# Top-32 attention with a transformer channel block: a deeper score lead, spread loads, one value transfer per job and an earlier vector transpose

## The chip, the core and the metric

The kernel runs on one core of one Trainium2 chip. A core has five engines that run their own instruction streams in order and meet only at semaphores: PE (TensorE, matrix products), DVE (VectorE), ACT (ScalarE), POOL (GpSimd) and SP (SyncE, which here only issues transfers). Transfers run on 16 DMA engines. The metric is the device time of one execution in microseconds, lower is better. The kernel before was run three times: 1655.44, 1657.19 and 1660.09 us, median 1657.19.

## The reference

The inputs are q, k, v of shape (8 batches, 8 heads, 576 rows, 64 columns) in float32, a layer-norm gain in float32 and two weights in float64.

```python
scores = (1/8) * q @ k.T                      # per batch and head, 576 x 576
kth = 32nd largest score of the row
attn = softmax(where(scores >= kth, scores, -1e9))
x = (attn @ v), heads side by side            # (8, 576, 512)
xn = (x - mean) / sqrt(var + 1e-6) * g_ln     # over the 512 columns
out = x + relu(xn @ w_ch1) @ w_ch2            # 512 -> 2048 -> 512
```

## The kernel before

**Units, groups, jobs, slots.** Two heads (a pair, `hp`) are worked on together. A *unit* is 128 query rows of both heads of a pair, two tiles of 128x576 scores; the fifth unit of a pair holds the remaining 64 rows of both heads in one tile (a *rest* unit). A *job* is one group of units of a batch and pair that share the values product. Batch 0 has the groups [0,1], [2,3], [rest], batch 1 [0,1], [2,3,rest], and batches 2 to 7 [0,1,rest], [2,3], always for four pairs in a row. That is 160 units in 68 jobs. The program is written out in one order by hand as a loop over *slots* `n` (line 1168), one unit further on in each slot, and every engine gets its instructions in that order.

**What a unit goes through.** `scores(u)` (L361) makes the scores on PE in four 288-column pieces and ACT copies them to `u.sc` (L367). `halve(u)` (L395) takes the larger and smaller of column pairs on DVE into `u.hi`, of which there are two buffers, and `u.lo`. `select(u, 0..3)` (L410) are four rounds of MAX8 and MATCH_REPLACE8 on DVE that find the 32nd largest. `prepare(u)` (L437) makes the threshold and bias, on DVE in the first 17 slots, on POOL afterwards, and reads `u.hi` for a later test (L452). `mask(u, t)` (L478) is a ReLU on ACT and a subtraction on POOL (L484); `weigh(u, t)` (L486) is the exponential on ACT. Then the weights must be transposed: on PE with copies on ACT (`turn`, L537), or, from batch 2 on and for all but the last unit of a group, by `move` (L518): two 128x512 transposes of 32x32 blocks on DVE (L524), a 512 KB write to memory (`turned`, L529) and four reads of 128 KB that bring it back as `pt` (L532). `values(g)` (L595) multiplies `pt` with the job's values: sixteen products with `vb` (L600) and two (L607) with a tile `ends` that holds the 64 rows of each head left over from 4x128, one head in each diagonal quarter and zeros elsewhere. In slot n the later part of the program works on `ex`, unit n-2 (n-1 in the first slots), and on the values of a group whose last unit is n-3.

**Loads.** `load(job, first, second)` (L282) brings k and q of a new pair as eight transfers of 72 KB in runs of 128 bytes (L289), right behind `turn_heads` (L311), whose DVE transposes free the single `kin` and `qin` buffers. Later groups of the same pair read the turned heads back from memory (`keep_heads`, `fetch_heads`). `load_values(job)` (L295) runs in the slot after the job's last unit was selected: two transfers of 128 KB into `vb` (L301) and two of 16 KB into one of two `ends` tiles (L305). All of these are issued by SP in program order, so a transfer that waits holds up every transfer behind it.

**The lead of the scores.** `due(n)` (L1076) lists the units whose scores are made at the start of slot n: n+1 up to slot 16, then n+2; slot 17 makes two. `halve` of unit n+1 comes in the middle of slot n.

**The channel block** is spread over the slots as filler for PE. `todo` holds its matrix products, and `fill()` (L262), called eight times in a slot, issues as many as the slot's `share` allows. `weights(n, phase)` (L205) converts the float64 weights piece by piece on ACT, POOL and DVE in the first 16 slots; before that is done there is little or no filler. `Later` (L238) keeps closures and runs them a number of `fill` calls afterwards.

The end of a slot of the kernel before, in program order (other statements left out):

```python
        fill()
        if parts: parts[-1]()
        if mk and len(mk.tiles) > 1 and not early: mask(mk, 1)
        fill()
        ... load_values(x.job) ...
        if u:
            select(u, 3)
        if moved:
            move(ex)
```

Of the kernel before, what the change touches and what calls it, by code (L numbers as in the profile page):

```python
# [11 lines left out]
FP32 = mybir.dt.float32  # L12
# [9 lines left out]
J = 4  # L22
# [7 lines left out]
def compute(  # L30
# [12 lines left out]
    nc = tc.nc  # L43
    P = nc.NUM_PARTITIONS
    B, H, S, D = q.shape
# [3 lines left out]
    JP = J * P  # L49
    R = S - JP  # L50
# [6 lines left out]
    def pool(name, bufs, **kw):  # L57
        return ctx.enter_context(tc.tile_pool(name=name, bufs=bufs, **kw))

    NV = 2  # L60
# [6 lines left out]
    vpool = pool("v", NV)  # L67
# [23 lines left out]
    def const(shape, name):  # L91
        return consts.tile(shape, FP32, tag=name, name=name)
# [9 lines left out]
        return mmps.tile([P, 512], FP32, tag="mm", name=name)  # L102


    ends = [const([P, P], f"ends{i}") for i in range(NV)]
    for t in ends:
        nc.gpsimd.memset(t[:], 0.0)
    if doubt is not None:
        watched = const([P, 34], "watched")
        nc.gpsimd.memset(watched[:], -1.0)  # L110
# [88 lines left out]
    queue = list(pieces)  # L199
# [5 lines left out]
    def weights(n, phase):  # L205

        now, before = batches.get(n, []), batches.get(n - 1, [])
        if phase == 0:  # L210
            for x in batches.get(n + 1, []):
                x.fetch()
            for x in now[0::2]:
                x.split()
        elif phase == 1:
            for x in before:
                x.join()
            for x in now[1::2]:
                x.split()
# [10 lines left out]
    def pop():  # L230
        kind, cost, run, may = todo.pop(0)
        assert not may or may()
        owed[0] -= cost
        run()
# [24 lines left out]

    sums_later, ends_later, stores = Later(), Later(), Later()  # L260

    def fill(least=0):  # L262
        tick[0] += 1
        ends_later.settle(END_AGE)
        fetch_forms(FETCH_AGE)
        owed[0] = min(owed[0] + share[0], 6.0)
        while todo and (not todo[0][3] or todo[0][3]()):
            if owed[0] < todo[0][1] / 2 and least <= 0:
                break
            least -= 1  # L270
            pop()
# [7 lines left out]
            self.b, self.hp = b, hp  # L279
            self.groups = groups  # L280

    def load(job, first, second):  # L282

        job.ins = {}
        for name, src, queue in (("k", k, first), ("q", q, second)):
            t = ldpool.tile([P, S], FP32, tag=name + "in", name=name + "in")
            for i in range(P // 32):
                head, d0 = 2 * job.hp + i * 32 // D, i * 32 % D
                queue.dma_start(  # L289
                    t[i * 32 : (i + 1) * 32, :].rearrange("b (n a) -> b n a", a=32),  # L290
                    src[job.b, head, :, d0 : d0 + 32].rearrange("(n b) a -> b n a", b=32),
                )
            job.ins[name] = t

    def load_values(job):  # L295
        vb = vpool.tile([P, 2 * J, D], FP32, tag="v", name="vb")
        job.ends = ends[jobs.index(job) % NV]
        for hh in range(2):
            rows = v[job.b, 2 * job.hp + hh]
            k0, end = (0, JP) if hh == 0 else (R, 0)  # L300
            nc.sync.dma_start(  # L301
                vb[:, hh * J : (hh + 1) * J, :],
                rows[k0 : k0 + JP, :].rearrange("(c p) d -> p c d", p=P),
            )
            nc.sync.dma_start(  # L305
                job.ends[hh * R : (hh + 1) * R, hh * D : (hh + 1) * D],
                rows[end : end + R, :],
            )
        job.v = vb

    def turn_heads(job):  # L311
        job.T = {}
# [48 lines left out]
    def scores(u):  # L361

        u.sc = scpool.tile([P, 2, S], FP32, tag="sc", name="sc")
        made = [score_half(u, s) for s in range(2)]
        for t in range(len(u.tiles)):
            for s in range(2):
                nc.scalar.copy(  # L367
                    u.sc[:, t, s * HALF : (s + 1) * HALF], made[s][t][:, 0:HALF]
                )
# [136 lines left out]
    def place_of(u):  # L506

        g = u.group  # L510
        if g.pt is None:
            g.pt = ptpool.tile([P, 2 * J + 1, GQ], FP32, tag="pt", name="pt")
            g.blocks = g.pt[:, 0 : 2 * J].rearrange("p c n -> p (c n)").rearrange(
                "p (i h c n) -> p h i c n", h=2, c=J, n=32
            )
        return sum(P for x in g.qts if x < u.qt) // 32

    def move(u):  # L518

        i0 = place_of(u)  # L520
        ni = P // 32
        blocks = u.sc[:].rearrange("p t n -> p (t n)")[:, 0 : 2 * JP]
        for t in range(2):
            nc.vector.transpose(  # L524
                blocks.rearrange("p (j t c n) -> p j t c n", j=ni, t=2, c=J)[:, :, t],
                u.e[:, t, t * R : t * R + JP].rearrange("p (c j k) -> p j c k", c=J, k=32),
            )
        hbm = hbmpool.tile([P, 2 * JP], FP32, tag="turned", name="turned")
        nc.sync.dma_start(hbm[:], blocks)  # L529
        for j in range(ni):  # L530
            to = u.group.pt[j * 32 : (j + 1) * 32, 0 : 2 * J].rearrange("k c n -> k (c n)")
            nc.sync.dma_start(  # L532
                to[:, i0 * 2 * P : (i0 + ni) * 2 * P].rearrange("k (i x) -> k i x", i=ni),
                hbm[:, j * 2 * P : (j + 1) * 2 * P].rearrange("(i k) x -> k i x", k=32),
            )
# [59 lines left out]
    def values(g):  # L595
        vb = g.job.v
        av = brief("av")
        for c in range(J):
            for h in range(2):
                nc.tensor.matmul(  # L600
                    av[h * D : (h + 1) * D, 0 : g.nq],
                    vb[:, h * J + c, :],
                    g.blocks[:, h, 0 : g.nq // 32, c, :],
                    start=(c == 0),
                    stop=False,
                )
        nc.tensor.matmul(  # L607
            av[:, 0 : g.nq], g.job.ends[:], g.pt[:, 2 * J, 0 : g.nq],
            start=False, stop=True,
        )  # L610
        g.av = av
# [316 lines left out]
            )  # L928

    PER_ROW = 1.71e-3  # L930
    SUM_AGE, END_AGE, FETCH_AGE, STORE_AGE = 7, 6, 10, 8
    blocks = []
    plain_done, formed, used, fetched = [None], [None], [], [0]

# [41 lines left out]
    def fetch_forms(age):  # L976
        if done(formed[0]):
            free = 4 + sum(tick[0] - x >= age for x in used)
            while fetched[0] < min(free, 8 * (len(blocks) - 1)):
                fetch_form()  # L980
# [11 lines left out]
    jobs = []  # L992
# [7 lines left out]
    units = []  # L1000
# [7 lines left out]
    N = len(units)  # L1008
    END = N + 6

    fresh = []
# [8 lines left out]
    CONVERTING = max(n for n in batches if batches[n]) + 2  # L1020
    EARLY = jobs[NHP].first
# [16 lines left out]
    for j in jobs:  # L1038
        if j.hp == NHP - 1:
            b = j.b  # L1040
            step = j.last + (3 if j.last < EARLY else 4)
# [34 lines left out]
    def due(n):  # L1076

        ahead = [] if n == 0 else [n + 1] if n < CONVERTING else [n + 2]  # L1080
        if n == CONVERTING:
            ahead = [n + 1, n + 2]
        return [units[i] for i in ahead if i < N]

    DVE_UNIT = 6.0 + 1.65 * low_rounds
    DVE_REST, DVE_MOVE, DVE_TURN = 0.58 * DVE_UNIT, 1.4, 1.45
# [3 lines left out]
    for j in jobs[1:]:  # L1090
        before = jobs[jobs.index(j) - 1]
        made = next(n for n in range(N) if units[j.first] in due(n))
        step = min(before.first, made - 1)
        if j.twin:
            fetches.setdefault(max(step - 1, 0), []).append(j)
        else:
            turns[step] = j
            keeps[step + 1] = j
# [43 lines left out]
                    left += sum(b.cost() for b in gives[m])  # L1142
        return max(0.0, even) / SLOTS

    recips, rows_of = {}, {}
    pairs_left, made_pair = list(range(4)), []

    def arrived(n, key, x):
# [19 lines left out]
    for n in range(END):  # L1168
# [9 lines left out]
        ex, g = after(n)  # L1178
        g = g if g and not g.quick else None
# [7 lines left out]
        moved = ex is not None and ex.moved  # L1187

        if ex and not early:
            weigh(ex, 0)  # L1190
        for x in due(n):
            scores(x)
        if g:
            values(g)
        if u:
# [42 lines left out]
        if n in turns:  # L1238
            turn_heads(turns[n])
            later = fresh.index(turns[n]) + 1  # L1240
            if later < len(fresh):
                load(fresh[later], nc.sync, nc.sync)
        if not quick:
            weights(n, 1)
        fill()
        if mk and not early:
            mask(mk, 0)
# [9 lines left out]
            select(u, 2)  # L1257
        for blk, i in rows_of.pop(n, []):
            blk.stats(i)
        for blk in gives.get(n - 2, []):  # L1260
            blk.inverse()
        if last and ex.group.sums is not None:
# [12 lines left out]
        for x in (u if n < EARLY else None, mk if n > EARLY else None):  # L1275
            if x and x is units[x.job.last]:
                load_values(x.job)
        if quick:

            values(quick)  # L1280
            take_values(quick)
            for den in recips.pop(n + 1):
                nc.vector.reciprocal(den, den)
            place(quick)
            weights(n, 0)
            weights(n, 1)
        if u:
            select(u, 3)
            if u.i < CONVERTING:
                prepare(u)  # L1290
        if moved:
            move(ex)
        for x in (g, quick):
            if x and x.job.hp == NHP - 1:
                for qt in x.qts:
# [7 lines left out]
        if late and late.job.hp == NHP - 1:  # L1303
            r = late.job.b // 2
# [62 lines left out]
```

## Time and profile before

| | |
|---|---|
| three runs | 1655.44, 1657.19, 1660.09 us; median 1657.19 |
| profiled execution | 1655.4 us, of which 1653.6 us from the first to the last instruction (the span) |
| mean granted TensorE clock | 0.963 |
| busy in the span | PE 1508.0, DVE 1334.3, POOL 1078.1, ACT 1067.4 us |
| transfers | 211.52 MB in 358951 packets, of which 250756 under 512 B; 16 engines 43.8% busy with SP's queue |
| value transfers | 136 of 128 KB, 136 of 16 KB |
| k and q transfers | 256 of 72 KB |

The profile is of one execution. "Busy" is the time in which an engine has an instruction at work; a wait is put down to the event that came last. Times inside the span are counted from its first instruction. The four engines depend on each other in every slot, so a busy share says less than the waits of a stretch do.

### The profile page before, as it was taken

Reading aid. Unit: us, or ns where it says so; the run is one execution under the profiler, and the core shown is the slowest. Engines: PE = TensorE matmul, PEld = TensorE weight load, DVE = VectorE, ACT = ScalarE, POOL = GpSimd, SP = SyncE. Lnnn points to the kernel's source line nnn. Section 1 sums busy time; section 2 is a strip of 40 time slices with the busy share of each in tenths; the row PEclk is TensorE's granted clock in tenths of the full one; section 3 lists DMA queues with packets and bytes.
Section 4 is the critical chain, followed back from the end, with each engine's and each line's share of the span. In section 5 each row is a group of like instructions: output and inputs, shape, how many; then the busy total and the mean of one; then the engine's idle time right before and its main releaser. Section 6 shows DMA issues by size and latency. Waiting matters only on the chain. (4 is left out here: it accounts for less than half of the span.)

```text
span 1653.6 us, 27426 instructions
## 1 busy us (share of the span) xinstructions
PE 1508.0 (91%) x7898; PEld 1132.7 (68%) x7898; DVE 1334.3 (81%) x3990; ACT 1067.4 (65%) x2712; POOL 1078.1 (65%) x1607
## 2 busy tenths in 40 slices
PE   2557898999989899899999999999989999999997
PEld 1235546677757677677777776677767777778886
DVE  6878998788989898899998988799879999884000
ACT  5777966677757676567666765677656766654311
POOL 4667866867657475667675866576756676856433
PEclk9768999999989999999999999999999999999999
DMA  7433434321454354554655444545554445442211
GB/s 199 110 100 114 130 81 119 114 66 46 109 167 152 109 168 118 162 153 118 185 160 168 126 126 135 163 138 138 158 158 150 134 135 181 149 131 71 91 32 53
DMA packets 358951, 211.52 MB, mean 128 GB/s; under 512 B 250756, under 2 KB 331144, under 8 KB 358792
## 3 DMA queue, kind: packets, MB, share of 16 engines
q1 hardware_dynamic: 354056, 209.10, 43.8%
q8 instruction: 65, 1.06, 0.3%
q10 hardware_dynamic: 4736, 0.59, 0.2%
q14 instruction: 94, 0.77, 0.2%
HBM read 145.62 MB, written 63.96 MB: 127 GB/s over the span
## 5 line engine op out<-in xcount | busy, mean ns | idle before, releaser
L484 POOL TENSOR_TENSOR e<-e,sc 128x576 f32<-128x576 f32 x288 | 412.4, 1435 | 419.4 <-ACT e L481 403.1
L745 PE MATMUL hps<-xT,w 128*128 128x256 f32 x2304 | 548.2, 384 | 2.5 <-ACT xT L707 2.5
L745 PEld LDWEIGHTS hps<-xT,w 128*128 128x128 f32 x2304 | 422.0, 191 | 72.8 <-issue 16.7
L429 DVE MAX8 m<-hi 128x8 f32<-128x296 f32 (+1 forms) x1152 | 464.3, 444 | 1.1
L415 DVE MATCH_REPLACE8 hi<-m,hi 128x288 f32<-128x288 f32 (+1 forms) x864 | 378.2, 444 | 0.0
L902 PE MATMUL ops<-w,h 128*128 128x256 f32 x1360 | 324.8, 381 | 0.0
L902 PEld LDWEIGHTS ops<-w,h 128*128 128x128 f32 x1360 | 247.7, 190 | 40.4 <-issue 6.9
L492 ACT ACTIVATE e<-e,m 128x576 f32<-128x576 f32 x288 | 224.8, 780 | 52.8 <-POOL e L484 52.4
L407 DVE TENSOR_TENSOR hi<-sc 128x576 f32<-128x576 f32 (+1 forms) x160 | 120.1, 751 | 157.4 <-POOL watched L452 135.7
L481 ACT ACTIVATE e<-sc,m 128x576 f32<-128x576 f32 x288 | 223.9, 781 | 14.6 <-POOL m L444 13.9
L367 ACT COPY sc<-scps 128x288 f32<-128x288 f32 x576 | 195.1, 406 | 38.6 <-PE scps L386 18.3
L600 PE MATMUL av<-pt,vb 128*64 128x256 f32 (+2 forms) x1088 | 159.4, 439 | 37.7 <-DMA pt<-turned 18.2
L768 ACT ACTIVATE h<-hps 128x512 f32<-128x512 f32 x144 | 86.5, 601 | 103.7 <-PE hps L745 102.9
L600 PEld LDWEIGHTS av<-pt,vb 128*64 128x64 f32 x1088 | 80.2, 149 | 106.5 <-issue 50.3
L386 PE MATMUL scps<-kT,late_qT 64*128 64x288 f32 (+3 forms) x832 | 129.0, 413 | 5.3 <-ACT pt L558 3.2
L902 PE MATMUL ops<-wt,s 128*128 128x256 f32 x544 | 129.2, 381 | 0.0
L546 PE MATMUL tp<-ident,e 128*128 128x128 f32 x576 | 93.9, 289 | 37.8 <-ACT e L492 37.4
L386 PE MATMUL scps<-kT,qT 64*128 64x288 f32 x512 | 94.8, 471 | 29.5 <-ACT sign L168 11.8
L408 DVE TENSOR_TENSOR lo<-sc 128x576 f32<-128x576 f32 (+1 forms) x160 | 120.9, 756 | 0.0
L546 PEld LDWEIGHTS tp<-ident,e 128*128 128x128 f32 x576 | 73.9, 148 | 65.7 <-ACT e L492 51.6
L421 DVE MAX8 hi<-lo 128x8 f32<-128x288 f32 x288 | 118.0, 446 | 0.0
L386 PEld LDWEIGHTS scps<-kT,late_qT 64*128 64x128 f32 (+1 forms) x832 | 72.0, 168 | 59.4 <-issue 23.5
(106 smaller groups left out, 1905.9 us busy)
## 6 DMA issues: line engine op xcount, KB each, us to landing
turned<-sc SPq DMA_DIRECT2D x72, 512.0 KB, 2.6
pt<-turned SPq DMA_DIRECT2D x288, 128.0 KB, 2.7
w<-forms SPq DMA_DIRECT2D x136, 256.0 KB, 3.8
vb<-in_v_dram SPq DMA_DIRECT2D x136, 128.0 KB, 3.1
raw<-in_moe_w_ch_dram SPq DMA_DIRECT2D x32, 512.0 KB, 4.3
kT<-kept SPq DMA_DIRECT2D x36, 288.0 KB, 3.2
kin<-in_k_dram SPq DMA_DIRECT2D x128, 72.0 KB, 2.3
kept<-kT SPq DMA_DIRECT2D x32, 288.0 KB, 2.9
```

Source lines behind the costliest of these rows:

```text
L367: nc.scalar.copy(u.sc[:, t, s * HALF : (s + 1) * HALF], made[s][t][:, 0:HALF])
L386: nc.tensor.matmul(ps[i * R : i * R + ql, o : o + width], qT[r, q0 : q0 + ql], kT[r, k0 : k0 + width], start=True, stop=True,)
L408: nc.vector.tensor_tensor(lo, a, b, ALU.min)
L415: nc.vector.match_replace(x, m[:, t, :], x, LOWEST)
L429: nc.vector.max(m[:, t, :], u.hi[:, t, 0:width])
L481: nc.scalar.activation(u.e[:, t], u.sc[:, t], AF.Relu, bias=u.edge[:, t : t + 1], scale=-STEEP)
L484: nc.gpsimd.tensor_tensor(u.e[:, t], u.e[:, t], u.sc[:, t], ALU.subtract)
L492: nc.scalar.activation(u.e[:, t], u.e[:, t], AF.Exp, bias=u.bias[:, t : t + 1], scale=-scale, accum_out=g.den[:, col : col + 1],)
L546: nc.tensor.transpose(ps[:, c * P : (c + 1) * P], u.e[:, t, c * P + t * R : (c + 1) * P + t * R], ident[:],)
L600: nc.tensor.matmul(av[h * D : (h + 1) * D, 0 : g.nq], vb[:, h * J + c, :], g.blocks[:, h, 0 : g.nq // 32, c, :], start=(c == 0), stop=False,)
L745: nc.tensor.matmul(ps[0][:, side * N : (side + 1) * N], w1[:, c, f * P : (f + 1) * P], self.xT[:, c, 0:N], start=(c == 0), stop=(c == NC - 1),
L902: nc.tensor.matmul(bank[name][:, 0:Q], a(j), rhs, start=first and j == 0, stop=(j == G - 1), skip_group_check=not first,)
```

## The change

The scores are made two units ahead from the first slot on (`due` returns unit n+2 always; unit 2 is scored in slot 0 behind the heads' transposes), and with them the heads' transposes and fetches of the first 17 slots move one slot earlier. The k and q loads of batch 1 and later are handed to a `Later` queue with `LOAD_AGE = 3`: the eight transfers are issued in pairs at the third to sixth `fill` call after `turn_heads`. `load_values` becomes one transfer of 288 KB in runs of 256 bytes, nine 128-row blocks of both heads, of which block J holds the last 64 rows of the first head and the first 64 of the second; a new function `fill_ends`, one slot later, copies the two halves of that block into a single `ends` tile on POOL. `move(ex)` goes from behind `select(u, 3)` to behind `select(u, 2)`, which also puts it ahead of `load_values` in the program.

```diff
--- before.py
+++ after.py
@@ -102,9 +102,8 @@
         return mmps.tile([P, 512], FP32, tag="mm", name=name)
 
 
-    ends = [const([P, P], f"ends{i}") for i in range(NV)]
-    for t in ends:
-        nc.gpsimd.memset(t[:], 0.0)
+    ends = const([P, P], "ends")
+    nc.gpsimd.memset(ends[:], 0.0)
     if doubt is not None:
         watched = const([P, 34], "watched")
         nc.gpsimd.memset(watched[:], -1.0)
@@ -259,8 +258,11 @@
 
     sums_later, ends_later, stores = Later(), Later(), Later()
 
+    loads = Later()
+
     def fill(least=0):
         tick[0] += 1
+        loads.settle(LOAD_AGE)
         ends_later.settle(END_AGE)
         fetch_forms(FETCH_AGE)
         owed[0] = min(owed[0] + share[0], 6.0)
@@ -279,34 +281,37 @@
             self.b, self.hp = b, hp
             self.groups = groups
 
-    def load(job, first, second):
+    def load(job, first, second, later=False):
 
         job.ins = {}
         for name, src, queue in (("k", k, first), ("q", q, second)):
             t = ldpool.tile([P, S], FP32, tag=name + "in", name=name + "in")
-            for i in range(P // 32):
+
+            def part(i, t=t, src=src, queue=queue):
                 head, d0 = 2 * job.hp + i * 32 // D, i * 32 % D
                 queue.dma_start(
                     t[i * 32 : (i + 1) * 32, :].rearrange("b (n a) -> b n a", a=32),
                     src[job.b, head, :, d0 : d0 + 32].rearrange("(n b) a -> b n a", b=32),
                 )
+
+            for i in range(P // 32):
+                if later:
+                    age = (4 * len(job.ins) + i) // 2
+                    loads.add(lambda i=i, part=part: part(i), -age)
+                else:
+                    part(i)
             job.ins[name] = t
 
     def load_values(job):
-        vb = vpool.tile([P, 2 * J, D], FP32, tag="v", name="vb")
-        job.ends = ends[jobs.index(job) % NV]
-        for hh in range(2):
-            rows = v[job.b, 2 * job.hp + hh]
-            k0, end = (0, JP) if hh == 0 else (R, 0)
-            nc.sync.dma_start(
-                vb[:, hh * J : (hh + 1) * J, :],
-                rows[k0 : k0 + JP, :].rearrange("(c p) d -> p c d", p=P),
-            )
-            nc.sync.dma_start(
-                job.ends[hh * R : (hh + 1) * R, hh * D : (hh + 1) * D],
-                rows[end : end + R, :],
-            )
-        job.v = vb
+
+        job.v = vpool.tile([P, 2 * J + 1, D], FP32, tag="v", name="vb")
+        rows = v[job.b, 2 * job.hp : 2 * job.hp + 2].rearrange("h s d -> (h s) d")
+        nc.sync.dma_start(job.v[:], rows.rearrange("(c p) d -> p c d", p=P))
+
+    def fill_ends(job):
+        for h in range(2):
+            r = slice(h * R, (h + 1) * R)
+            nc.gpsimd.tensor_copy(ends[r, h * D : (h + 1) * D], job.v[r, J, :])
 
     def turn_heads(job):
         job.T = {}
@@ -599,13 +604,13 @@
             for h in range(2):
                 nc.tensor.matmul(
                     av[h * D : (h + 1) * D, 0 : g.nq],
-                    vb[:, h * J + c, :],
+                    vb[:, h * (J + 1) + c, :],
                     g.blocks[:, h, 0 : g.nq // 32, c, :],
                     start=(c == 0),
                     stop=False,
                 )
         nc.tensor.matmul(
-            av[:, 0 : g.nq], g.job.ends[:], g.pt[:, 2 * J, 0 : g.nq],
+            av[:, 0 : g.nq], ends[:], g.pt[:, 2 * J, 0 : g.nq],
             start=False, stop=True,
         )
         g.av = av
@@ -928,7 +933,7 @@
             )
 
     PER_ROW = 1.71e-3
-    SUM_AGE, END_AGE, FETCH_AGE, STORE_AGE = 7, 6, 10, 8
+    SUM_AGE, END_AGE, FETCH_AGE, STORE_AGE, LOAD_AGE = 7, 6, 10, 8, 3
     blocks = []
     plain_done, formed, used, fetched = [None], [None], [], [0]
 
@@ -1077,10 +1082,7 @@
 
 
 
-        ahead = [] if n == 0 else [n + 1] if n < CONVERTING else [n + 2]
-        if n == CONVERTING:
-            ahead = [n + 1, n + 2]
-        return [units[i] for i in ahead if i < N]
+        return units[n + 2 : n + 3]
 
     DVE_UNIT = 6.0 + 1.65 * low_rounds
     DVE_REST, DVE_MOVE, DVE_TURN = 0.58 * DVE_UNIT, 1.4, 1.45
@@ -1090,7 +1092,7 @@
     for j in jobs[1:]:
         before = jobs[jobs.index(j) - 1]
         made = next(n for n in range(N) if units[j.first] in due(n))
-        step = min(before.first, made - 1)
+        step = max(min(before.first, made - 1), 0)
         if j.twin:
             fetches.setdefault(max(step - 1, 0), []).append(j)
         else:
@@ -1142,7 +1144,7 @@
                     left += sum(b.cost() for b in gives[m])
         return max(0.0, even) / SLOTS
 
-    recips, rows_of = {}, {}
+    recips, rows_of, ends_due = {}, {}, {}
     pairs_left, made_pair = list(range(4)), []
 
     def arrived(n, key, x):
@@ -1188,8 +1190,9 @@
 
         if ex and not early:
             weigh(ex, 0)
-        for x in due(n):
-            scores(x)
+        if n:
+            for x in due(n):
+                scores(x)
         if g:
             values(g)
         if u:
@@ -1239,9 +1242,13 @@
             turn_heads(turns[n])
             later = fresh.index(turns[n]) + 1
             if later < len(fresh):
-                load(fresh[later], nc.sync, nc.sync)
+                load(fresh[later], nc.sync, nc.sync, n >= EARLY)
+        if n == 0:
+            scores(units[2])
         if not quick:
             weights(n, 1)
+        if n in ends_due:
+            fill_ends(ends_due.pop(n))
         fill()
         if mk and not early:
             mask(mk, 0)
@@ -1257,6 +1264,8 @@
             select(u, 2)
         for blk, i in rows_of.pop(n, []):
             blk.stats(i)
+        if moved:
+            move(ex)
         for blk in gives.get(n - 2, []):
             blk.inverse()
         if last and ex.group.sums is not None:
@@ -1275,6 +1284,7 @@
         for x in (u if n < EARLY else None, mk if n > EARLY else None):
             if x and x is units[x.job.last]:
                 load_values(x.job)
+                ends_due[n + 1] = x.job
         if quick:
 
             values(quick)
@@ -1288,8 +1298,6 @@
             select(u, 3)
             if u.i < CONVERTING:
                 prepare(u)
-        if moved:
-            move(ex)
         for x in (g, quick):
             if x and x.job.hp == NHP - 1:
                 for qt in x.qts:
```

## Prediction

> **What bounds the kernel now.** I read the page first, then busy time by stretch, then the waits of the stretches that stood out, then the timeline around the longest of them.
>
> ```profile
> PE 1508.0 (91%) x7898; PEld 1132.7 (68%) x7898; DVE 1334.3 (81%) x3990; ACT 1067.4 (65%) x2712; POOL 1078.1 (65%) x1607
> PE   2557898999989899899999999999989999999997
> ```
>
> PE is idle for 1653.6 - 1508.0 = 146 us, and most of it lies in the first six slices, before the channel block gives PE filler. From there on PE's work is fixed, so time is won or lost only where PE idles. Busy time by stretch (PE, PE weight loads, DVE, ACT, POOL, then clock, DMA share, GB/s):
>
> ```profile
> 60.00:126.00 66.00, 36.02 (x136) 20.02 (x133) 48.90 (x155) 49.78 (x113) 44.50 (x35) 0.61 0.37 106
> 126.00:205.00 79.00, 64.04 (x312) 43.99 (x311) 73.48 (x203) 64.95 (x149) 63.58 (x54) 0.91 0.39 123
> ...
> 439.00:1500.00 1061.00, 1019.31 (x5433) 777.06 (x5433) 950.66 (x2854) 698.48 (x1829) 699.13 (x1109) 0.98 0.50 145
> ```
>
> Waits of 60 to 126 us (total, times, longest), DVE's and then ACT's:
>
> ```profile
> DVE hi L407 <- ACT sc L367: 15.2, 5, 3.7
> ...
> ACT e L492 <- POOL e L484: 12.9, 12, 2.8
> ACT sc L367 <- PE scps L386: 3.8, 7, 0.7
> ```
>
> DVE does wait for scores, but ACT's 49.8 us of work and its two waits add up to 66.5 of 66 us: ACT is the pace there. In 126:205 DVE is, with 93%.
>
> In 439:1500, where `move` runs, PE idles 41.7 us. PE's waits after 260 us, and the SP queue ahead of one of the longest:
>
> ```profile
> PE av L600 <- DMA pt<-turned: 18.2, 7, 5.1
> PE av L600 <- DMA kept<-late_qT: 7.8, 2, 4.5
> PE av L600 <- DMA dr<-den: 6.0, 1, 6.0
> ```
>
> ```profile
> 478.16 2.06 SPq L289 DMA_DIRECT2D qin<-in_q_dram  x4
> 480.27 0.50 SPq L301 DMA_DIRECT2D vb<-in_v_dram  x1
> 480.81 0.52 SPq L305 DMA_DIRECT2D ends<-in_v_dram  x1
> 481.37 0.59 SPq L301 DMA_DIRECT2D vb<-in_v_dram  x1
> 482.00 0.51 SPq L305 DMA_DIRECT2D ends<-in_v_dram  x1
> 482.62 0.53 SPq L529 DMA_DIRECT2D turned<-sc  x1
> 485.45 1.75 SPq L532 DMA_DIRECT2D pt<-turned  x4
> ```
>
> DVE's transposes (start 478.02, 1.29 long) had ended at 479.3; the write left 3.3 us later behind eight head loads (0.5 us each) and four value loads. PE's values began at 489.83 after a wait of 4.98. The other long ones look alike: with smaller waits ahead of values they sum to 37.7 us, nearly all of PE's idle time here.
>
> **The change, part by part.** Let T be the end of the two transposes of `move` before.
>
> *Earlier turn.* `select(u, 3)` costs two MAX8 of 0.45 us, so the transposes end at T - 0.9, and the threshold of u comes at T instead of T - 1.3. Its readers are `prepare` on POOL (POOL waited for DVE's MAX8 only 8.0 us in all) and through it ACT's masks; I count 0, and at most 1.3 us in some slots if POOL arrives early.
>
> *Loads spread.* On SP only two of the eight head loads stay ahead of the write, issued before the transposes end; the other six and the value load fall behind write and reads. The weights now arrive at T - 0.9 + 2.8 (write) + 1.75 (four issues) + 2.7 (landing) = T + 6.4, where the 479.3 case had T + 10.5. By itself that takes away about all of the 37.7 us.
>
> *Value load behind the turn.* This is the price. SP waits for the write before it issues the reads, and the values sit behind that, with two k and two q loads (2.0 us) ahead of them in slots with head loads. For 288 KB in 256-byte runs no row exists: 128 KB in such runs takes 2.3 us at the least, 3.1 in the median, 6.5 at most, and 288 KB in long runs (kT<-kept) 3.2. I take 3.4, nearest to the last, between 2.3 and 6.5. They land at T - 0.9 + 2.8 + 1.75 + 2.1 + 0.1 + 3.4 = T + 9.3 with head loads and T + 7.2 without. PE needs them at the first product of the group. Counting PE's arrival (start minus wait) from T in the 48 slots that load values behind a move, the 22 with head loads split: ten arrive at T + 10 or later and wait for neither, twelve at T + 5.5 to 9.1 (5.8 and 5.5 in the first two, which waited 3.0 and 5.0). Waiting until T + 9.3 these twelve lose 23 us, the sum of 9.3 less each arrival; before, that group of slots lost 30.7. Slots without head loads lost 7.0 and will lose about 2. So the stall is mostly handed from `pt` to `vb`: 25 us in place of 37.7, a gain of 12.7. With a landing of 2.3 it is 23, with 4.5 about 0.
>
> *Ends through POOL.* 136 copies of 64x64; the nearest row (L633, 128x64) has 238 ns, so 32 us of POOL work, at 66% busy in this stretch, hidden. They also wait until PE is through with the group before, whose values come a slot earlier in the program: 0. But `fill_ends` waits for the value load, and behind it on POOL stand the subtractions of that slot's masks:
>
> ```profile
> 814.94 0.19 POOL L445 TENSOR_SCALAR m<-m 128x2 f32<-128x2 f32 x1
> 818.34 1.41 POOL L484 TENSOR_TENSOR e<-e,sc 128x576 f32<-128x576 f32 x1 [3.21 <-ACT e L481]
> ```
>
> Here T was 815.1; the copies now end at T + 9.8 = 824.9, so the subtraction starts 6.6 us late. Worked through in the same way, the 48 slots have 125 us of late subtractions. ACT's exponential behind them has 1.3 us of slack on average, and POOL then lets DVE go on (`watched`, two `hi` buffers). From the end of one move to the next through POOL: 10.2 (T + 9.3 counted from T - 0.9) + 0.7 copies + 2.8 subtractions + 0.4, then DVE's halve, rest rounds and second move, next unit, heads' transposes and move, 14.5: 28.6 us. DVE alone needs about 25 (two full units of 8.2, a rest unit of 4.4, two moves, the heads); the groups now take 24.6 to 31.6, 27.8 on average. Those at 24.6 to 25.2 are stretched, which PE takes up where it is behind anyway. I put 4 us for that and 4 for ACT's late copies; bounds 0 and 25.
>
> The Trainium skill (GPSIMD Engine Reference, section Key points) adds that GpSimd shares its SBUF interfaces with VectorE and contends with DVE instructions that have two SBUF inputs. This trace agrees at 97.88 us: of two subtractions that took 3.34 us the first ran beside DVE's halve, 1.9 us against the usual 1.43. By this rule the 136 copies would slow DVE's halves by at most their own 32 us, of which DVE's idle 110 us would hide most.
>
> *Fewer transfers.* Four issues of 0.5 us become one: SP gains 1.6 us per job, counted above. The Trainium skill (DMA: Bandwidth & Descriptors, section Anatomy of one DMA) gives a fixed 2 us per DMA plus its bytes at 436 GB/s; by it 288 KB would land in an estimated 2.7 us, and the gain would be near its upper end. The 288 KB row above, at 3.2, speaks for a bit more.
>
> *Scores two ahead.* In 60:126 DVE's 15.2 us vanish, but ACT sets the pace and its order is unchanged. What can shrink is ACT's 12.9 us behind POOL: the first subtraction of a slot ran beside DVE's halve there (3.34 us for two that elsewhere take 1.43 each); apart from it, it would give back 0.47 us in each of five slots, 2.5 us. The bounds are 0, since no instruction is added on ACT, and 11: the waits for POOL cannot fall under 1.1 us a slot (two subtractions of 1.43 against a mask of 0.78 and an exponential of 0.97), which leaves 7.4 of the 12.9, and the 3.8 for scores might go whole. DVE's lead dies in slots 8 and 9, where it waits for ACT's `den` and `x` (2.2 and 3.0 us), so 126:205 gains nothing. Unit 2's scores keep their time (PE started them at 25.3 us, when the heads were turned), and heads turned one slot earlier cost DVE the same; both 0.
>
> Sum on the profiled execution: 1655.4 - 12.7 + 8 - 2.5 = 1648.2, 7 us less. It stands 1.8 below the median of the runs; against 1657.19 I forecast 1650.
>
> **Rivals.** *Both waits go:* if the values land in 2.3 us and no group is stretched, 23 and the early 2.5 to 11 come off 1657.2: 1623 to 1632. For it: idle POOL in front of most subtractions; against: the early arrivals at T + 5.5.
> *POOL becomes the path (slower):* `fill_ends` holds POOL until the values land. Where a group's 28.6 us exceed what PE needs, everything shifts; with a landing of 4.5 the loop is 29.7, 1.9 over the average of 17 such groups, 32 us, of which PE's own lateness may cover two thirds, and the stall gain is gone: 1662 to 1687, with the early 2.5 off. It decides from a landing of about 4 us.
> That the change doesn't do what it says: the program order shows all four parts.
>
> **Numbers.** Forecast case 0.45, own range 1642 to 1660; both waits go 0.25; POOL 0.30. A measurement tells about 0.3% (5 us) from no change: faster is below 1652.2, slower above 1662.2. Faster 0.27 + 0.25 = 0.52, same 0.13 + 0.01 = 0.14, slower 0.05 + 0.29 = 0.34. The range 1630 to 1674 leaves out the better half of the second and the tail of the third.
>
> **What would show it.** Right: `turned` is issued within 0.1 us of DVE's transposes in all slots, PE's waits at L600 are put down to `vb`, about 25 us, and POOL shows a new wait of `ends` for `vb`, 165 us if it comes as early as now. DVE's wait for `sc` in 60 to 126 is gone and slots there last 12 us still. Wrong: those early slots shrink below 11 us, or PE's idle time in 439:1500 falls under 20 us or grows over 60.

## The result and the profile after

The changed kernel takes 1684.42 us in the median of four runs (1680.44 to 1685.43); beside it the kernel before took 1657.83. The ratio is 1.0156, with a 95% interval of 1.0134 to 1.0178: slower by 26 us. The forecast was 1650 with a range of 1630 to 1674, so it was wrong in sign and in range; the result lies in the range of the slower rival, 1662 to 1687.

The page of the changed kernel, engine totals and PE's forty slices:

```profile
PE 1517.3 (90%) x7898; PEld 1137.5 (68%) x7898; DVE 1339.3 (80%) x3990; ACT 1067.6 (63%) x2712; POOL 1118.3 (66%) x1742
PE   3557889999979998999899999999999999999997
```

The span is 1682.1 us. PE idles 164.8 us of it against 145.6 before, and the same 7898 products take 9 us longer. By stretch (PE, PE weight loads, DVE, ACT, POOL, then clock, DMA share, GB/s):

```profile
60.00:126.00 66.00, 38.03 (x147) 21.16 (x145) 61.58 (x163) 51.69 (x118) 44.36 (x41) 0.62 0.36 107
126.00:205.00 79.00, 62.45 (x310) 44.15 (x309) 74.53 (x198) 63.03 (x144) 67.12 (x58) 0.91 0.41 131
439.00:1500.00 1061.00, 999.87 (x5311) 757.19 (x5308) 929.95 (x2808) 686.92 (x1804) 714.63 (x1185) 0.98 0.50 143
```

In the last stretch PE idles 61 us where it idled 42. The page's groups for the values' products and for the copies of the ends show the two new waits:

```profile
L605 PE MATMUL av<-pt,vb 128*64 128x256 f32 (+2 forms) x1088 | 164.4, 450 | 49.7 <-DMA qin<-in_q_dram 24.4
L314 POOL COPY ends<-vb 64x64 f32<-64x64 f32 x136 | 34.0, 250 | 219.1 <-DMA vb<-in_v_dram 180.9
```

PE waits 49.7 us ahead of the values (37.7 before), and the products behind these waits are longer too, 164.4 us against 159.4. The releaser named is the last transfer by the profile, here a q load behind `vb` on the same queue; what PE waited for is seen in the order of SP. One of the longest waits, at the move whose transposes ended at 670.80:

```profile
670.83 0.34 SPq L534 DMA_DIRECT2D turned<-sc  x1
673.52 1.73 SPq L537 DMA_DIRECT2D pt<-turned  x4
675.30 0.97 SPq L292 DMA_DIRECT2D kin<-in_k_dram  x2
676.31 1.04 SPq L292 DMA_DIRECT2D qin<-in_q_dram  x2
677.45 0.45 SPq L976 DMA_DIRECT2D w<-forms  x1
677.99 0.41 SPq L309 DMA_DIRECT2D vb<-in_v_dram  x1
```

The write goes out 0.03 us after the transposes, as forecast, and the values follow 7.2 us after them, behind four head loads and a piece of the channel weights. GpSimd's queue at the same place (the bracket is the idle time ahead of an instruction):

```profile
681.85 0.52 POOL L314 COPY ends<-vb 64x64 f32<-64x64 f32 x2 [8.27 <-DMA vb<-in_v_dram]
682.45 2.77 POOL L489 TENSOR_TENSOR e<-e,sc 128x576 f32<-128x576 f32 x2
685.18 0.20 POOL L457 TENSOR_TENSOR watched<-hi,m 128x2 f32<-128x2 f32 x1
```

and VectorE's and PE's:

```profile
685.41 0.76 DVE L412 TENSOR_TENSOR hi<-sc 128x576 f32<-128x576 f32 x1 [4.75 <-POOL watched L457]
```

```profile
682.04 3.46 PE L605 MATMUL av<-pt,vb 128*64 128x320 f32 x16 [3.71 <-DMA qin<-in_q_dram]
```

One late transfer makes two engines late here. PE starts at 682.04, 11.2 us after the transposes. GpSimd's copies wait 8.27 us; the two mask subtractions, then `watched`, then VectorE's next halving come in a row behind them, and VectorE loses 4.75 us, on which the next move depends. The sums of such waits in 439 to 1500 us, ends, masks' exponential, halves:

```profile
POOL ends L314 <- DMA vb<-in_v_dram: 176.3, 36, 11.9
ACT e L497 <- POOL e L489: 144.9, 62, 9.4
DVE hi L412 <- POOL watched L457: 126.2, 58, 7.2
```

Before, the last two rows (with L492 and L407) had 16.4 and 94.2 us for ACT and VectorE.

### The profile page after: what moved, and what is told of

Same layout as the page of the kernel before. It is cut to its first block, busy times and chain, and to the rows that moved or that the text cites. A ratio compares the mean times of both kernels' runs of the same rounds, so it can differ in the third digit from the quotient of the medians.

```text
span 1682.1 us, 27351 instructions
## 1 busy us (share of the span) xinstructions
PE 1517.3 (90%) x7898; PEld 1137.5 (68%) x7898; DVE 1339.3 (80%) x3990; ACT 1067.6 (63%) x2712; POOL 1118.3 (66%) x1742
## 5 line engine op out<-in xcount | busy, mean ns | idle before, releaser
L434 DVE MAX8 m<-hi 128x8 f32<-128x296 f32 (+1 forms) x1152 | 458.2, 444 | 0.2
L412 DVE TENSOR_TENSOR hi<-sc 128x576 f32<-128x576 f32 (+1 forms) x160 | 124.5, 778 | 183.5 <-POOL watched L457 178.4
L605 PE MATMUL av<-pt,vb 128*64 128x256 f32 (+2 forms) x1088 | 164.4, 450 | 49.7 <-DMA qin<-in_q_dram 24.4
L314 POOL COPY ends<-vb 64x64 f32<-64x64 f32 x136 | 34.0, 250 | 219.1 <-DMA vb<-in_v_dram 180.9
L605 PEld LDWEIGHTS av<-pt,vb 128*64 128x64 f32 x1088 | 84.4, 154 | 121.0 <-issue 84.2
```

The lines of the kernel that those rows point to most:

```text
L412: nc.vector.tensor_tensor(hi, a, b, ALU.max)
L434: nc.vector.max(m[:, t, :], u.hi[:, t, 0:width])
L605: nc.tensor.matmul(av[h * D : (h + 1) * D, 0 : g.nq], vb[:, h * (J + 1) + c, :], g.blocks[:, h, 0 : g.nq // 32, c, :], start=(c == 0), sto ...
```

## The experiments

The kernel before ran beside each set, and its medians there lay between 1654.65 and 1659.58; so times are compared as ratios to it, and "+5 us" below is the ratio less 1, times 1657.2. The first four kernels take single parts: the order of value load and move, the hold on GpSimd, the lead by itself, and the form of the value load.

**Values first.** `load_values` is issued ahead of the move, at the same place in the program.

```diff
+        for x in (u if n < EARLY else None, mk if n > EARLY else None):
+            if x and x is units[x.job.last]:
+                load_values(x.job)
+                ends_due[n + 1] = x.job
         if moved:
             move(ex)
```

> The changed kernel with load_values put ahead of move in the slot, so that SP issues the value transfer before it waits for the transposes; all else as changed. Theory A (the value transfer behind the move lands about 10.8 us after the transposes and holds PE at vb and POOL at the ends copies): the ends copies' wait for vb falls from 181 us to under 40, PE's waits ahead of values in the slots with moves from about 50 us to under 15, and the time to 1635 to 1648 us. Theory B (the copies on POOL and their place ahead of the mask subtractions cost the time whenever the values land): the time stays above 1668. Theory C (the deeper lead of the scores costs it): it stays above 1675.

Measured 1625.65 us, ratio 0.982 (0.9781 to 0.9858): 56 us less than the changed kernel, 30 less than before, and 9 under the range of theory A.

```profile
L605 PE MATMUL av<-pt,vb 128*64 128x256 f32 (+2 forms) x1088 | 151.1, 423 | 16.3 <-ACT e L497 9.3
```

PE's stall falls to 16.3 us, the products to 151.1, and GpSimd's wait for `vb` from 180.9 to 1.4 us. The order of two statements turns the change from a loss into a gain.

**Ends behind the masks.** `fill_ends` goes behind the second mask of its slot.

> The changed kernel with fill_ends moved behind the slot's second mask, so that POOL waits for the values only after the subtractions; the value transfer stays behind the move. Theory A (PE waits for vb itself, and POOL's hold comes on top): PE's waits ahead of values stay at 35 us or more, POOL's late subtractions go; 1662 to 1676 us. Theory B (POOL's hold of the subtractions is the whole cost): back to 1650 or less. Theory C: no change from 1684.

Measured 1680.8 us, ratio 1.0149 (1.0107 to 1.0192): within the interval of the changed kernel. That was theory C's number, but the next experiment finds no cost of the lead; theory A's signs came (PE waits 45.4 us ahead of the values, the hold on the masks is gone), its time did not. The wait was handed on (439 to 1500 us first):

```profile
ACT e L497 <- POOL e L489: 16.8, 17, 2.6
```

```profile
PE av L612 <- POOL ends L314: 19.8, 10, 4.0
```

The second row, of the whole span, is new: the ends now come so late that PE waits for them at the last product of a group, for 19.8 us. So this run could not show that the hold is cheap.

**The lead alone**, on the kernel before: `due` returns unit n+2, and unit 2 is scored in slot 0.

> The kernel before with the deeper lead of the scores alone (and the heads' transposes and fetches that move with it). Theory A: 1653 to 1660 us; 2.5 us gained before the fourth group's values (at 125.4 instead of 128.0 us, as in the changed kernel), nothing lost afterwards. Theory C: 1665 or more, with the loss in the slots of the rest units of batch 0 (190 to 240 us), where the changed kernel loses 5.7 us.

Measured 1652.67 us, ratio 0.9977 (0.9955 to 1.0): -4 us, with an interval that reaches 0. Theory C fell. The fourth values come 2.1 us earlier than before, but the slots of the rest units of batch 0 (191 to 238 us) lose 4, so that the twelfth values come later (262.6 us against 260.4); later stretches win more.

**Four value loads**, as before, with two `ends` tiles, behind the early move; no copies on GpSimd.

> The changed kernel with the four value transfers and the two ends tiles of the kernel before, without copies on POOL; they stay behind the move. Theory A (PE waits for the values because of their place in the queue): PE's waits ahead of values stay, the last of the four transfers leaves 1.6 us later than the single one but is smaller; POOL's wait for vb is gone; 1662 to 1678 us. Theory B (POOL's hold is the whole cost): 1652 or less.

Measured 1650.53 us, ratio 0.9971 (0.9953 to 0.999): 31 us better than the changed kernel, where theory A had expected at most 22: theory B's number, though PE still waits 24.5 us ahead of the values. Either the one large landing or GpSimd's part cost more than thought. The next set was to part these, and took the other side of the change apart. First, the one transfer cut in two:

```diff
+        for c0, c1 in ((0, J), (J, 2 * J + 1)):
+            nc.sync.dma_start(
+                job.v[:, c0:c1, :],
+                rows[c0 * P : c1 * P, :].rearrange("(c p) d -> p c d", p=P),
+            )
```

> The changed kernel with the one value transfer cut in two at its fourth block (128 KB and 160 KB, one more issue on SP, about 1 us behind the first); all else is kept, GpSimd's two copies and the single ends tile too. Theory A (what counts is when the last values land: 10.3 to 11.3 us after the move's transposes in the tight slots of the changed kernel, 9.2 to 10 with four transfers, and with the values ahead of the move PE waits for pt alone, 7.5 to 8): two smaller transfers land together earlier than one large, so most of what four transfers gave back comes: 1652 to 1664 us. Theory B (the form costs, not the landing: GpSimd's copies and the single ends tile): no change, 1680 to 1688.

Measured 1680.24 us, ratio 1.015 (1.0126 to 1.0174). Two parts bring nothing: PE's stall falls to 39.1 us, but its products grow to 170.1 and GpSimd still waits 190.9 us, for the second part. The time is theory B's, but the run does not decide against theory A: in the slots with head loads the last part landed 10.7 us after the transposes in the median, and the one transfer 10.8, so the earlier landing that theory A counted on did not come about.

**Four loads ahead of the move** (the fourth experiment with the order of the first):

> The early move, the lead and the spread loads with the values in four transfers as before, now issued ahead of the move. Theory A: with the values out of the way of pt the form does not matter, 1620 to 1632 us, as with the one transfer ahead of the move (1625.7). Theory B: the form costs in either place, so another 20 to 30 us go: 1595 to 1612.

Measured 1620.14 us, ratio 0.9794 (0.9762 to 0.9826), -34 us: the fastest kernel of this study. Against the one transfer ahead of the move (0.982) the difference lies inside the intervals. The form matters much less where the values come early.

```profile
439.00:1500.00 1061.00, 1042.12 (x5615) 801.12 (x5614) 967.85 (x2890) 714.02 (x1866) 721.79 (x1153) 1.00 0.51 149
```

PE idles 19 us in this stretch, and it gets 304 more of its products done there than the changed kernel.

**Ends by transfers in the same slot**, two of 16 KB behind the one of 288 KB, in place of the copies. With one `ends` tile it is refilled a slot early here, before the previous job's last group has used it, so some groups are multiplied with the next job's rows.

> The changed kernel with the one transfer of 288 KB kept, and the ends tile filled by two transfers of 16 KB right behind it on SP's queue in place of GpSimd's two copies. Theory A: PE still waits for the one large landing: 1676 to 1690 us. Theory B: GpSimd's part was the cost, 1648 to 1660.

Measured 1657.66 us, ratio 1.0012 (0.9991 to 1.0033): 24 us better than with the copies, while PE's stall is still 35.7. That spoke for GpSimd, but a product that waits for the next job's rows is no clean witness.

**The move alone**, on the kernel before: move and value loads go behind the third selection round, values first, nothing else.

> The kernel before with one thing changed: the move stands behind the third selection round, with the four value transfers still ahead of it (no early lead, no spread of the loads, four transfers, two ends tiles). Theory A: the early move in this order is what carries the gain; the bunched head loads delay some of it: 1624 to 1640 us. Rival C (the loads spread over slots carry it, since the bunch held the move's SP issues): 1645 to 1657.

Measured 1654.25 us, ratio 0.9981 (0.9962 to 1.0): -3 us, where I had expected 17 to 33; the number is rival C's. SP's queue ahead of the transposes that ended at 656.7 tells why:

```profile
653.56 2.73 SPq L289 DMA_DIRECT2D kin<-in_k_dram  x3
656.39 2.06 SPq L289 DMA_DIRECT2D qin<-in_q_dram  x4
658.55 0.44 SPq L971 DMA_DIRECT2D w<-forms  x1
659.04 0.47 SPq L301 DMA_DIRECT2D vb<-in_v_dram  x1
...
661.36 0.53 SPq L529 DMA_DIRECT2D turned<-sc  x1
```

The write left 4.7 us behind the transposes. Half a microsecond per issue, SP was still at the head loads when they ended; an earlier move only waits longer in this queue.

The third set tested the hold on GpSimd by a different lever, and the spread of the loads. First, the small subtraction goes to VectorE (the indices of `hi` and `thr` are left out here):

```diff
-        eng = nc.vector if u.i < CONVERTING else nc.gpsimd
+        eng = nc.vector
         eng.tensor_tensor(
             watched[:, c : c + nt], u.hi[...], u.thr[...], ALU.subtract
```

> The changed kernel with the one small subtraction that reads the halves for the later test (watched from hi and m) on VectorE in place of GpSimd, from the fourth unit on. Theory D (GpSimd's copies of the ends wait for vb, the watched subtraction of the next slot stands behind them in GpSimd's order, and VectorE may write the next halves only after it: 178 us of such waits against 124 with the ends filled by transfers): VectorE's waits for watched go, 1655 to 1670 us, the rest above that being held mask subtractions and late values. Rival A (PE's wait for the late values is the cost): 1676 to 1690.

Measured 1682.17 us, ratio 1.0147 (1.013 to 1.0164), next to nothing and rival A's number. Two things speak against a simple reading. The masks are still held (ACT waits 180 us for GpSimd in the whole span, as in the changed kernel). And VectorE pays for the cure:

```profile
L457 DVE TENSOR_TENSOR watched<-hi,m 128x2 f32<-128x2 f32 (+1 forms) x160 | 68.0, 425 | 0.6
```

Of these 160, 143 came from GpSimd, 61 us of new work at 425 ns each on average.

The tenth experiment also puts the copies behind the masks:

> The same on top of GpSimd's copies behind the slot's mask subtractions: neither masks nor halves are held by the copies any more. Theory D: 1650 to 1662, as with the ends filled by transfers (1657.7). Rival A: 1674 to 1688, no better than the copies behind the masks alone (1680.8).

Measured 1668.39 us, ratio 1.0052 (1.0033 to 1.007). With neither masks nor halves held, 17 us of the changed kernel's time go, in spite of VectorE's 60 us of extra work and 20.3 us in which PE waits for late ends. The time lies between theory D's range and rival A's. One reading is that each hold alone keeps the loop long, which would be why the second and the ninth experiment showed so little; it is not shown. In the second experiment VectorE's wait for `watched` had also fallen, to 100.6 us in 439 to 1500, near the 94.2 of the kernel before, and the tenth takes away even those 94.

**The spread alone**, on the kernel before (`loads` and `LOAD_AGE` only), and **spread and early move**, values first in four loads, no lead:

> The kernel before with one thing changed: from the fourth unit on the head loads are spread over the slots, as in the changed kernel; the move stays at the end of the slot, no lead, four value transfers ahead of the move. Theory E (SP's order was the delay: eight head loads in a bunch and four value transfers stood ahead of turned, which SP issued 0.7 to 5.1 us after the transposes): 1622 to 1638 us. Rival (the move's place matters as much, the transposes about 0.9 us earlier): 1640 to 1652.

> The spread and the early move with the values ahead of it, four value transfers, no early lead: the kernel of 1620.1 us without its lead. If the lead is worth what it was alone: 1621 to 1628. Rival: the lead costs in the rest units' slots (4 us lost between 191 and 238 us) what it brings early: 1614 to 1620.

Measured 1644.03 us, ratio 0.9914 (0.9897 to 0.9931), and 1627.17 us, ratio 0.9816 (0.9799 to 0.9832). Spread -14, move -3, both -30: the two need each other. The write left over 1 us behind the transposes in 15 of 72 moves before, in 17 with the early move alone, 11 with the spread alone, and in 3 with both. The lead is worth 4 us on top (1620.1), as by itself, but here the intervals overlap. Both guesses at a single carrier, the move and the spread, were wrong.

The last set asked whether GpSimd's wait, its work or the landing costs. In the second of these kernels the copies read `ident`, a constant tile, in place of `job.v[r, J, :]`, so its sums lack the rows of `ends`; in the first and the third `fill_ends` issues, at its own place in the next slot, two transfers into `ends`.

> The changed kernel with GpSimd's two copies replaced, at their own place in the next slot, by two transfers of 16 KB into the one ends tile; the transfer of 288 KB stays behind the move. Theory D (GpSimd's wait for vb holds the masks and the watched subtraction): 1650 to 1662. Rival A (late values alone): 1676 to 1690.

> The changed kernel with GpSimd's two copies reading a constant tile in place of vb: the same copies at the same place, but nothing in them waits for the transfer (the ends rows of the values are left out of the sum). Theory D: the wait is the cost, 1650 to 1664. Rival F (the 32 us of copies themselves, or what they hold in GpSimd's order): 1674 to 1688.

> A version that might beat all so far: the one transfer of 288 KB ahead of the early move, and the ends by two transfers in the next slot, so that SP issues one transfer and not four ahead of turned, and GpSimd copies nothing. Theory D with E: 1614 to 1622, at or below the four transfers ahead of the move (1620.1) and below the one with GpSimd's copies (1625.7). Rival: the ends transfers delay other issues on SP, 1622 to 1630.

Measured 1668.58 us, ratio 1.0096 (1.0073 to 1.0119); 1664.1 us, ratio 1.0062 (1.0043 to 1.0081); and 1658.25 us, ratio 1.0017 (1.0001 to 1.0033). The second is the clean one: the same copies at the same place, and only the wait is gone.

```profile
DVE hi L412 <- POOL watched L457: 92.5, 44, 6.8
ACT e L497 <- POOL e L489: 21.7, 22, 2.6
```

These are the waits of 439 to 1500 us, back at 92.5 and 21.7 from 126.2 and 144.9, and 16 us of time go with them (1.0156 less 1.0062; the two intervals leave 9 to 22). That is theory D, at the edge of its range, and rival F fell. The other 10 us over the kernel before stay, with PE's stall of 44.0 us. The first, free of copies, gives 10 of the 16, between both ranges: PE's stall is 41.3 us, and now the ends come late through SP's queue (PE waits 4.5 us for them at the last product).

The third, meant as an improvement, missed both its ranges: it lost 33 us against its sister with the copies (0.982). PE's wait for it, 439 to 1500 us:

```profile
PE av L615 <- DMA ends<-in_v_dram: 31.3, 12, 4.8
```

The two small transfers stand in SP's queue behind the next slot's head loads and stores, and arrive after `pt` and `vb`. This is the mistake of the change itself over again, with 32 KB in place of 288.

## Why the prediction was wrong

**What held.** `turned` was issued 0.03 us behind the transposes in all 72 moves. GpSimd's new wait for `vb` was forecast at 165 us and measured at 180.9. The late mask subtractions were worked out at 125 us; ACT's wait for GpSimd grew by 128.5 us in 439 to 1500. The early lead was right: 60 to 126 us holds 51.69 us of ACT work and two waits of 10.3 and 3.7 us, so ACT is the pace there still, VectorE's waits for scores in it, 15.2 us before, are gone, and the gain at the fourth values was 2.5 us as put. That the lead is worth 4 us by the end is luck as far as the forecast goes: by itself it had lost the early gain again at the twelfth values, and where the 4 us come from is open. That early move and spread take away "about all of the 37.7 us" was right too: with the values first and no lead, 14.3 us of stall remain, and 30 us of time go. This is the size of the rival "both waits go" (1623 to 1632), but by another order of the program than the one that was changed. One sign of being wrong was met: PE's idle time in 439 to 1500 us grew to 61, over the 60 named.

**The step that failed first** is the stall of 25 us in place of 37.7. It rested on a landing of 3.4 us, read off 288 KB in long runs; the page has

```profile
vb<-in_v_dram SPq DMA_DIRECT2D x68, 288.0 KB, 3.9
```

Counted from the end of the transposes, the values were to be there after 10.2 us in slots with head loads. In the 13 such slots of 439 to 1500 with a wait PE started after 11.3 on average: SP issued the load 7.1 us after the transposes and not 6.75, as in some slots a piece of the channel weights stood ahead of it, the landing took half a microsecond more, and the rest is the step from landing to PE. Thirteen times 1.1 us is 14 of the 20 us by which these slots exceed the 23 forecast (they lost 42.7); the rest is one slot more than the twelve and PE coming 8.0 us after the transposes on average, earlier than I had let some of them come. The slots without head loads lost 6.9 us and not 2, 4.0 of it in one where SP issued the load 7.3 us after the transposes. In place of a gain of 12.7 stands a stall 12 us longer than before, and 5 us more in the products, which ran longer at a lower clock (last section).

On that estimate the Trainium skill (DMA: Bandwidth & Descriptors, section Anatomy of one DMA) was further off than the row I took: 2.7 us by its formula against 3.9 here, in runs of 256 bytes. The section gives the formula for transfers that GpSimd issues; this one is issued by SP.

**The second step** is the 8 us put for GpSimd's hold; taking away its wait alone brought 16. The chain was right link by link (`vb`, ends, subtractions, `watched`, halves, the next move), and its length nearly: ten such loops of 439 to 1500 us, from one move with head loads to the next, took 28.1 to 30.9 us, 29.7 on average where 28.6 was put, and 28.1 on average before. What was wrong, as far as can be told, was to take the groups that run faster than 28.6 us as covered by PE being behind anyway. PE was waiting for the same transfer in many of these slots, so its lateness could cover little; that this is the whole of the difference is argued, not shown. The rival's point of decision, a landing of about 4 us, was nearly met by the median of 3.9; it deserved the higher chance. The two steps are off by 30 us (12.7 and 12 of stall, 5 of products) and by 8, against 33 us between forecast and result; waits do not add up to time exactly.

**A step that was not there:** edits weighed one by one. Move and spread are worth 3 and 14 us alone and 30 together, and the value load, put down as a price of a few microseconds, decides over all of it: from its place ahead of the move to the one behind costs 29 us with four loads (0.9794 to 0.9971) and 56 with one and the copies (0.982 to 1.0156).

The sum in time, by ratios: spread and early move -30, lead -4, values behind the move +29, one load with copies that do not wait +15, their wait +16, together +26. How the 15 divide between the larger landing and GpSimd's 34 us of copies is open: cutting the transfer in two left GpSimd's wait as it was, and both ways of filling the ends by transfers moved other waits. For the landing speaks PE's stall, 44.0 us there against 24.5 with four loads. The single `ends` tile shows no cost: in that kernel the copies wait for PE nowhere in 439 to 1500 us.

## What to carry to other kernels

On a queue that issues in order, an edit is judged by what it puts ahead of the transfer that ends the next wait, so a load with no condition of its own belongs ahead of a store that waits and of the loads that wait for that store. A small copy that waits for a transfer holds all that stands behind it on its engine; ask what that is, and who waits for it two engines on. When two engines wait for one transfer, price both waits, and look where a lifted wait goes: in this case taking GpSimd's away brought 16 of the 26 us, and handing it on to PE next to nothing.

## What was not expected of the hardware

The granted clock of 439 to 1500 us was 0.98 before and after the change and 1.00 with four loads ahead of the move; the 1088 values products took 439 and 450 ns on average, and 423 there. In this case a wait thus costs more than its idle time: from the changed kernel to that one PE's stall fell by 36.9 us and these products by another 13.1, with the same products in the same number. The trace shows why. The clock record of that stretch of the changed kernel has ten pieces at 0.5, of 3.4 or 6.8 us and 51 us in all, each beginning 2.1 to 4.8 us after one of PE's waits began; with four loads ahead of the move there are two, 7 us in all. One of the ten, at the wait of 5.8 us that ended at 652.5 (columns as in the stretches above):

```profile
649.00:655.80 6.80, 3.31 (x14) 1.72 (x16) 2.52 (x9) 1.55 (x5) 3.38 (x6) 0.50 0.60 144
```

Wholly at full clock the products of L605 took 407 ns in the changed kernel and 412 in the fastest, wholly inside such a piece 745 and 738; 111 fell inside in the one and 18 in the other.

The Trainium skill (TensorE: Matmul & The Clock Gate, section HAM oscillation) names idle gaps of more than about 3.4 us as what lowers PE's clock. This case agrees in kind, but not with a bound at that length: in the 17 profiles of this study, 439 to 1500 us, a piece at 0.5 began in or within 2.5 us behind 10 of 21 waits of 2 to 2.5 us, 25 of 35 of 2.5 to 3, 23 of 26 of 3 to 3.5, and 57 of 58 longer ones. No run varied the length of a gap alone.

The small subtraction took 195 ns on GpSimd in the median of the changed kernel, and 425 on average on VectorE in the ninth experiment, but that average hides two cases:

```profile
L457 DVE TENSOR_TENSOR watched<-hi,m x160: 142/250/1352, 28.0 to 1541.2; 128x2 f32<-128x2 f32 x128, 128x1 f32<-128x1 f32 x32
```

(shortest, median and longest, in ns). Of the 143 that had moved, the 51 that started while GpSimd had nothing at work took 143 to 160 ns, less than on GpSimd. All 69 that took over 200 ns ended within 23 ns of the end of a GpSimd instruction beside them, most of them behind the mask subtractions. So the small operation was not dear on VectorE; it waited there for GpSimd's long ones.
